# mLSTM cell and exact-GELU block: the values of two batches placed next to each other in the Down stages

## The chip, the cores and the metric

The kernel runs on one core of one Trainium2 chip. The metric is the device time of one execution in microseconds; lower is better. All matmuls are in 32-bit floating point, and each one that the program names appears as two weight loads and two matmul records in the profile.

## What is computed

The first half is an mLSTM cell over 4 batches, 8 heads, 768 time steps and a head size of 40. The second half is a two-layer block with an exact GELU, from 320 features to 2048 and back, applied to the 3072 rows that the first half gives.

```python
for t in range(S):
    m_new  = maximum(f[t] + m, i[t])
    f_stab, i_stab = exp(f[t] + m - m_new), exp(i[t] - m_new)
    C = f_stab * C + i_stab * outer(v[t], k[t])      # 40 x 40 for each batch and head
    n = f_stab * n + i_stab * k[t]
    y[t] = sigmoid(o[t]) * (C @ q[t]) / maximum(abs(n @ q[t]), 1)
x   = y.transpose(0, 2, 1, 3).reshape(3072, 320)
h   = x @ w_in                                        # 320 -> 2048
out = (0.5 * h * (1 + erf(h / sqrt(2)))) @ w_out      # 2048 -> 320
```

## The kernel before

**Chunks and stages.** The sequence is cut into 6 chunks of 128 time steps. Within a chunk the cell is written in its parallel form: scores between all pairs of time steps, weighted, times the values, plus what the carried state gives. The kernel runs in stages. FRONT computes the gates, the cell of chunks 0 and 1 and the products of chunk 0. Then, for c = 1 to 4, an Up stage computes the hidden layer of chunk c, and a Down stage computes the second product of chunk c while the cell of chunk c + 1 runs between its pieces. The text calls these Down stages 1 to 4. A last Up stage and its own product close the kernel. In the profile, the Down stages lie at 155.7 to 197.9, 224.6 to 268.9, 295.6 to 339.2 and 365.8 to 406.6 us.

**What sets the order.** The order within FRONT and DOWN is written out by hand as a string of words; `play` goes through the words and emits the instructions of each. Each engine has its own queue and works through it in that order; it waits where an operand or a buffer is not ready. A word can put instructions on several engines, and on SP, which issues the transfers. No scheduler changes the order.

**The words that matter here.** The digit is the batch.

- `F`: one product step of the Down stage, 8 matmuls of 128 x 128 by 160 columns (L1065). There are 14 in a stage; below they are called F1 to F14 in their order. Two steps fill one bank of PSUM (accumulator memory), then a copy or an addition takes it out (L1076, L1080, L1086).
- `V`: `values`. 8 heads times 4 quarters, 32 matmuls with weights of 128 x 32 and 41 columns (L657), into one bank of tag "a" of the pool `ps_mm`, which has two. One addition on VectorE (DVE) follows (L665). Reading the batch's last inputs also puts loads for the next chunk on a list, `later_loads`, which the next Up stage issues in order.
- `S2`: `scores_two`, the scores of batches 2 and 3 (L555), then 8 multiplications on VectorE (L561). Its four banks are the two of tag "a" and two of tag "tr". `S0` is the same for batches 0 and 1.
- `C2`, `h2`: `read_two` (L610) and `update_two` (L621, and L630, L634, L636 off TensorE) for batches 2 and 3; `C0`, `h0` for batches 0 and 1.
- `K`, `Q`: transposes of keys and queries on VectorE (L489), from the tile `blocks`, which a transfer fills.
- `Z`: pieces of sums of weights on VectorE (L775), in stage 1 only. `N`: two subtractions on VectorE (L1091) that F11 and F12 need.
- `M`, `W`, `G`: mask on GpSimd (POOL, L441), exponentials on ScalarE (ACT, L467), the output gate on ScalarE (L473).
- `Y`: `finish`, on ScalarE, GpSimd and VectorE (L672 to L679). `X`: `turn_y`, 3 transposes on TensorE (L697) and a copy on ScalarE (L707). `R`: `split_x`, two operations on VectorE (L720, L721).

Of the kernel before, what the change touches and what calls it, by code (L numbers as in the profile page):

```python
# [34 lines left out]
    K K B8 F J K F F J K F F F R0 X1 J J K F J F K X2 F J  # L35
    K F J Y3 K F R1 e J F Z B9 B10 F X3 R2 Z R3 F p"""
DOWN = """
    F Z M0 Z W0 F M1 L3 W1 S0 C0 M2 F B3 K2 F G1 h0 Q2 D3 G2 V0 K3 Z W2 F Q3 V1 M3 G0 Z F G3 W3 S2 C2 h2 F Y0 F V2
    F Y1 X0 N Y2 F R0 V3 F X1 F Y3 j X2 R1 F R2 X3 R3 F"""


@with_exitstack
# [1154 lines left out]
```

## Time and profile before

| What | Value |
|---|---|
| median of 3 runs | 465.99 us (465.16 to 466.73) |
| the profiled execution | 465.24 us, span 463.2 us from first to last instruction |
| TensorE matmul (PE), busy | 452.3 us, 98% of the span |
| TensorE weight load (PEld), busy | 400.5 us, 86% |
| VectorE (DVE), busy | 336.7 us, 73% |
| ScalarE (ACT), busy | 253.0 us, 55% |
| GpSimd (POOL), busy | 79.0 us, 17% |
| granted TensorE clock | 1.00 throughout |
| the four Down stages | 42.2, 44.3, 43.6 and 40.7 us |

The busy time of matmuls overlaps from one to the next, so a single row's length is more than what it adds to the path; the step from one start to the next start is what counts. Weight loads run beside matmuls. "Issue" stands for time in which an engine waited for nothing that the profile shows.

### The profile page before, as it was taken

The numbers are of one execution on the slowest core, as the hardware profiler recorded it, in microseconds if no ns is written. First come the engines' busy times: TensorE is split into PE (matmuls) and PEld (weight loads), VectorE is DVE, ScalarE is ACT, GpSimd is POOL, SyncE is SP. The second block draws the span as 40 slices with busy tenths as digits, with TensorE's granted clock in tenths as the row PEclk, the third lists the DMA queues.
The fourth block names the chain that finished last, engine by engine and source line by source line (L and its number), as shares of the span: only waits on it lengthen the run. The fifth ranks groups of instructions, "written<-read, shape, count | busy, mean of one in ns | idle before, by whom it ended". The sixth has DMA issues, their size and how long they took to land.

```text
span 463.2 us, 13002 instructions
## 1 busy us (share of the span) xinstructions
PE 452.3 (98%) x5348; PEld 400.5 (86%) x5348; DVE 336.7 (73%) x737; ACT 253.0 (55%) x545; POOL 79.0 (17%) x120
## 2 busy tenths in 40 slices
PE   8899999999999999999998999999999999999996
PEld 7687888867788899988898998899998899988996
DVE  7899879798868996746577654587664685699950
ACT  6986999854354784203694113594123594257701
POOL 3002120000020232300443200353301411200000
PEclk9999999999999999999999999999999999999999
DMA  9997993268777650057972056973049960210001
GB/s 168 203 215 184 199 224 105 64 135 226 111 201 153 120 98 5 24 115 149 200 124 33 11 118 139 208 112 61 1 87 172 164 106 3 79 38 0 1 1 57
DMA packets 174875, 51.11 MB, mean 110 GB/s; under 512 B 154752, under 2 KB 168352, under 8 KB 174816
## 3 DMA queue, kind: packets, MB, share of 16 engines
q1 hardware_dynamic: 174496, 49.95, 52.9%
q8 instruction: 42, 0.69, 0.6%
q10 hardware_dynamic: 320, 0.33, 0.2%
q14 instruction: 17, 0.14, 0.1%
HBM read 45.47 MB, written 10.03 MB: 120 GB/s over the span
## 4 chain that ended last, share of the span: by engine, by line
PE 89%; DVE 4%; DMA 2%; SPq 1%; POOL 1%; issue 1%; ACT 0%; DVEq 0%; POOLq 0%
PE po L1065 25%; PE pu L949 23%; PE po L1044 7%; PE pu L806 6%; PE pu L960 6%; PE po L919 6%; PE ph L657 4%; PE ps L555 3%; PE pu L812 2%; PE px L697 2%; PE pf L610 1%; PE ps L539 1%; SPq L155 1%; PE pf L577 1%; PE pt L517 1%
## 5 line engine op out<-in xcount | busy, mean ns | idle before, releaser
L1065 PE MATMUL po<-w_out,g 128*128 128x160 f32 x512 | 76.2, 303 | 0.0
L964 ACT ACTIVATE g<-pu 128x512 f32<-128x512 f32 x64 | 32.2, 618 | 77.4 <-PE pu L960 77.4
L1065 PEld LDWEIGHTS po<-w_out,g 128*128 128x128 f32 x512 | 70.3, 190 | 2.2 <-ACT g L964 1.3
L467 ACT ACTIVATE W<-W,aT 128x128 f32<-128x128 f32 x128 | 39.2, 389 | 2.1 <-POOL W L441 2.0
L949 PE MATMUL pu<-x_hi,w_in_hi 128*128 128x512 f32 x160 | 39.0, 387 | 0.0
L441 POOL TENSOR_SCALAR_AFFINE_SELECT W<-W 128x1024 f32<-128x1024 f32 (+2 forms) x20 | 25.0, 1258 | 79.1 <-DMA W<-M_d 70.4
L949 PE MATMUL pu<-x_lo,w_in_lo 128*128 128x512 f32 x160 | 37.8, 379 | 0.0
L1065 PE MATMUL po<-w_sums,sums 128*128 128x160 f32 x256 | 36.9, 302 | 0.0
L1065 PEld LDWEIGHTS po<-w_sums,sums 128*128 128x128 f32 x256 | 35.0, 190 | 0.4
L1044 PE MATMUL po<-w_out,g 128*128 128x320 f32 x128 | 35.2, 433 | 0.0
L686 ACT COPY y_rest<-ob 128x128 f32<-128x128 f32 x16 | 4.8, 298 | 55.4 <-DVE ob L679 29.2
L949 PEld LDWEIGHTS pu<-x_hi,w_in_hi 128*128 128x128 f32 x160 | 29.5, 189 | 5.7 <-ACT g L964 1.3
L949 PEld LDWEIGHTS pu<-x_lo,w_in_lo 128*128 128x128 f32 x160 | 30.2, 189 | 4.3
L526 POOL TENSOR_TENSOR vw<-vb,ewT 128x328 f32<-128x328 f32 x12 | 9.2, 780 | 138.4 <-DMA vb<-in_v_dram 99.2
L1044 PEld LDWEIGHTS po<-w_out,g 128*128 128x128 f32 x128 | 24.0, 190 | 9.6
L949 PE MATMUL pu<-x_all,w_mid 128*128 128x512 f32 x80 | 30.3, 379 | 0.0
L949 PE MATMUL pu<-x_all,w_in_mid 128*128 128x512 f32 x80 | 30.3, 379 | 0.0
L806 PE MATMUL pu<-first_x,w_in 128*128 128x256 f32 x128 | 28.9, 381 | 0.0
L793 DVE TENSOR_TENSOR sums<-g 128x512 f32<-128x512 f32 x16 | 13.6, 853 | 18.3 <-ACT g L964 18.3
L806 PEld LDWEIGHTS pu<-first_x,w_in 128*128 128x128 f32 x128 | 23.8, 190 | 3.3 <-DVE w_in L388 0.2
L765 DVE TENSOR_TENSOR w_in_mid<-w_in_hi,w_in_lo 128x512 fp32r<-128x512 f32 x20 | 13.7, 686 | 16.5 <-PE pu L949 16.5
L561 DVE TENSOR_TENSOR W<-ps,W 128x256 f32<-128x256 f32 (+1 forms) x48 | 17.9, 413 | 10.7 <-PE ps L555 9.0
(196 smaller groups left out, 963.2 us busy)
## 6 DMA issues: line engine op xcount, KB each, us to landing
W<-M_d SPq DMA_DIRECT2D x16, 512.0 KB, 5.6
bits<-in_moe_w_in_dram SPq DMA_DIRECT2D x20, 256.0 KB, 4.5
bits<-in_moe_w_out_dram SPq DMA_DIRECT2D x16, 320.0 KB, 3.2
blocks<-kq_d SPq DMA_DIRECT2D x32, 128.0 KB, 3.3
ob<-in_o_gate_dram SPq DMA_DIRECT2D x24, 160.0 KB, 4.4
out_dram<-o_sb SPq DMA_DIRECT2D x36, 80.0 KB, 2.0
kq_d<-in_k_dram SPq DMA_DIRECT2D x32, 80.0 KB, 2.5
kq_d<-in_q_dram SPq DMA_DIRECT2D x32, 80.0 KB, 2.5
```

Of the source, the lines that this page charges most:

```text
L441: nc.gpsimd.affine_select(out=x, in_=x, compare_op=OP.is_ge, fill=1.0e30, base=base, pattern=[[0, H], [1, x.shape[2]]], channel_multiplier=-1)
L467: nc.scalar.activation(out=W[n][:, h, :], in_=src, func=AF.Exp, scale=-1.0, bias=aT[:, self.c, r:r + 1])
L555: nc.tensor.matmul(ps[i][hip][halves[x ^ i], p, t], kT[i][r, p, halves[x]], qT[i][r, p, t], start=True, stop=True)
L561: nc.vector.tensor_tensor(out=w[r, :, t], in0=ps[i][hip][r, :, t], in1=w[r, :, t], op=OP.mult)
L657: nc.tensor.matmul(ph[r, h, :], Pm[:, h, r], vb[turn_of(n)][:, h, :], start=True, stop=True)
L806: nc.tensor.matmul(banks[-1][e][:, i - i0, :], in_tile(i, x)[:, e, i % 2 * P:(i % 2 + 1) * P], first_x[:, x, t0:t1], start=(x == 0 and i = ...
L919: nc.tensor.matmul(in_pairs(po[t]), x[:, t * L:(t + 1) * L], in_turns(w), start=(f, k) == first, stop=(f, k) == last, skip_group_check=True)
L949: nc.tensor.matmul(in_pairs(pus[i][e]), w[k][:, e, i * P:(i + 1) * P], in_turns(x[:, k, :]), start=(n == 0 and k == 0), stop=False, skip_g ...
L960: nc.tensor.matmul(in_pairs(pu[e]), w[r, i // 2, i % 2 * P:(i % 2 + 1) * P], in_turns(x[r, NX, :]), start=False, stop=(n == 2), skip_group ...
L964: nc.scalar.activation(out=g.t[:, HF * e + i, :], in_=pu[e], func=AF.Gelu, scale=4097.0)
L1044: nc.tensor.matmul(po[b], g.t[:, f, b * L:(b + 1) * L], w_out[:, f, :], start=(f == 0), stop=(f == NF - 1))
L1065: nc.tensor.matmul(bank[k][:, t, :], lhs(j, t), rhs(j), start=(first and t == 0 and j == 0), stop=(t == 1 and j == HF - 1), skip_group_che ...
```

## The change

Only the string DOWN changes. The word `V1` moves from behind `F5` and `Q3` to the place right behind `V0`; the word `V3` moves from behind `F10` and `R0` to the place right behind `V2`. The string is played in all four Down stages, so eight groups of 32 matmuls stand elsewhere in TensorE's order, eight additions elsewhere in VectorE's, and in `later_loads` the entries of `V3` come before that of `X0`. No instruction is added and none removed.

```diff
 DOWN = """
-    F Z M0 Z W0 F M1 L3 W1 S0 C0 M2 F B3 K2 F G1 h0 Q2 D3 G2 V0 K3 Z W2 F Q3 V1 M3 G0 Z F G3 W3 S2 C2 h2 F Y0 F V2
-    F Y1 X0 N Y2 F R0 V3 F X1 F Y3 j X2 R1 F R2 X3 R3 F"""
+    F Z M0 Z W0 F M1 L3 W1 S0 C0 M2 F B3 K2 F G1 h0 Q2 D3 G2 V0 V1 K3 Z W2 F Q3 M3 G0 Z F G3 W3 S2 C2 h2 F Y0
+    F V2 V3 F Y1 X0 N Y2 F R0 F X1 F Y3 j X2 R1 F R2 X3 R3 F"""
```

On TensorE the first junction of a stage was V0 F5 V1 F6 S2 and is now V0 V1 F5 F6 S2. The second was V2 F9 X0 F10 V3 F11 and is now V2 V3 F9 X0 F10 F11.

## The prediction

> **What bounds the kernel now.** I read the page's busy times first, then its chain of waits.
>
> ```profile
> PE 452.3 (98%) x5348; PEld 400.5 (86%) x5348; DVE 336.7 (73%) x737; ACT 253.0 (55%) x545; POOL 79.0 (17%) x120
> ...
> PE 89%; DVE 4%; DMA 2%; SPq 1%; POOL 1%; issue 1%; ACT 0%; DVEq 0%; POOLq 0%
> ```
>
> TensorE holds the path: what shortens its row of instructions counts in full, and so does every hole in it. Next the timeline of PE where Down stage 1 reaches batches 0 and 1 (start, length, line):
>
> ```profile
> 167.16 0.81 PE L621 MATMUL pf<-vw,kb 128*40 128x41 f32 x32
> 167.90 0.81 PE L657 MATMUL ph<-vb,W 128*32 128x41 f32 x64
> 168.65 2.44 PE L1065 MATMUL po<-w_out,g 128*128 128x160 f32 x16
> 171.02 0.81 PE L657 MATMUL ph<-vb,W 128*32 128x41 f32 x64
> ```
>
> L621 is the end of h0, L657 is V0 and V1, L1065 between them is the product step F5; F6 follows V1 and S2 starts at 174.13. By differences of starts V0 takes 0.74, F5 2.37, V1 0.74, F6 2.37. There is no hole. A V is dense: 64 weight loads and 64 matmuls in 0.74 us, where an F has 32 such instructions in 2.37.
>
> The same timeline in stage 3 has holes. A bracket gives the idle time before a row, and "issue" means that nothing in the profile was being waited for:
>
> ```profile
> 310.93 0.56 PE L657 MATMUL ph<-vb,W 128*32 128x41 f32 x34
> 311.89 0.50 PE L657 MATMUL ph<-vb,W 128*32 128x41 f32 x30 [0.40 <-issue]
> ...
> 316.08 0.49 PE L610 MATMUL pf<-state,qT 64*64 64x41 f32 x18
> 316.99 0.90 PE L610 MATMUL pf<-state,qT 64*64 64x41 f32 x46 [0.42 <-issue]
> ```
>
> Start to start the two holes are 0.60 and 0.65 us; stage 2 has one of 0.65 (247.28 to 247.94, in h2), and the cell in FRONT one of 0.64 (92.68 to 93.31, in a V). I counted TensorE's records (loads, matmuls, its own waits) from the trace's start: these four stops fall on instructions 2,241, 5,825, 7,361 and 7,617, which are 193 above a multiple of 256, all four. The page's third part gives the unit:
>
> ```profile
> q8 instruction: 42, 0.69, 0.6%
> ```
>
> 42 packets of 16 KB for 10,788 instructions, so a packet is a block of 256. So the stops are TensorE waiting for its own instructions. In the DMA view the block ahead of each stop starts at 90.83, 245.65, 309.62 and 314.55 and is copied in 1.10, 0.93, 0.88 and 1.09; TensorE goes on at 93.31, 247.94, 311.89 and 316.99. From the end of the copy that is 1.38, 1.36, 1.39 and 1.35 us: **a block can be used about 1.37 us after its copy ends**. A block is asked for some 300 instructions before its first is needed (copies never start earlier than that, and 0.5 to 3.5 us after TensorE passes that point). 300 instructions with an F among them last over 4 us; three dense groups in a row don't.
>
> **The change, part by part.** No instruction is added or removed; in each of four Down stages V1 goes in front of F5 and V3 in front of F9.
>
> *Fewer changes of shape (gain).* F5 and F6 in one run take 4.54 (as the runs of two in all stages do) instead of 2 x 2.37: -0.20. V0 is followed by V1 instead of F5. Its 64 matmuls last 0.615 from first start to last start, and the step to F5 is 0.13. The step V to V is not in the trace: the nearest row with equal tile shapes (L555 to L610) has 0.04, a change of shape (L621 to L657) 0.13, the pitch inside a V 0.01. I take 0.04: V0 costs 0.65, -0.09. First junction -0.29 (bounds -0.20 and -0.32). At the second, V2 likewise -0.09, F10 goes from 2.27 to 2.18 because F11 follows it, F11 from 2.28 to 2.18 because no V precedes it: -0.28.
>
> *Where the first junction's gain is lost.* In stage 2 S2 waits:
>
> ```profile
> 244.46 1.45 PE L555 MATMUL ps<-qT,kT 64*64 64x128 f32 x56 [1.00 <-DVE far L665]
> ```
>
> The releaser is V1's addition on VectorE, queued behind K3 and Q3, which came late since K2 waited for its transfer. With V1 in front of K3 the addition comes first and Q3 last: the same three pieces of work end at 244.41 as before, and S2 needs Q3. TensorE only waits longer: 0 in stage 2 (bound -0.29, if the stop in h2 shrinks).
>
> *Instruction blocks (cost).* Instruction numbers within the moved pieces shift, so a boundary meets other work. I laid the new order over the count.
> Stage 1: instruction 3,521 (13 x 256 + 193) is now the 117th of V1's 128. V1 starts at 167.90 + 0.65 = 168.55 and reaches it at 169.1. Its block is asked for in h0, before anything changes; it starts at 168.58 and is copied in 1.43, so it is there at 168.58 + 1.43 + 1.37 = 171.38. Before, V1 came to the same number at 171.41, just late enough. Stop: 2.27 us (1.75, if the distance from the copy's start, 2.27 at the shortest stop, is what counts). From V0 to S2: 0.65 + 0.56 + 2.27 + 0.17 for V1's rest + 4.54 = 8.19 against 6.23: +1.96.
> Stage 3: instruction 7,361 is the 104th of V1, reached at 307.82 + 0.65 + 0.50 = 308.97; its block is usable at 311.89, as the trace shows: a stop of 2.92. V0 to S2: 0.65 + 0.50 + 2.92 + 0.24 + 4.54 = 8.85 against 6.87 (which held the old 0.60): +1.98. The next boundary (7,617, in C2) is reached at 318.3; its block was usable at 316.99, so the old 0.65 goes: -0.65.
> Stages 2 and 4: the boundaries lie in S2 (5,569, usable 1.37 after 239.77) and early in V1 (9,153, reached at 378.2; its block, started at 373.88 and copied in 0.88, is usable at 376.1). No stop.
> Second junctions: V2 and V3 follow two F and nothing dense. The tightest is stage 1, instruction 4,289, early in F10, some 4.4 us after V2's start, where its block was asked for; that block took 1.1 to start, 1.31 to copy and 1.37 to be used, 3.8 together. No stop, at 0.6 us of slack.
>
> The Trainium skill has a rule against these stops. Its page "Runtime: NRT & Kernel Launch", section "Instruction fetch mechanics", says that instructions come in 16 KiB blocks of 256, that TensorE holds 2,048 of them, and that crossing a block is "mostly hidden". The block size agrees with the 42 packets; the four stops, about 300 instructions after a request, speak against both the depth and the hiding. By that rule the sum would be the gains alone, which is the first rival.
>
> *Queues.* On VectorE V1's addition (0.46 to 0.50) now stands before K3, the pieces of Z and Q3. In stage 4 Q3 ends at 381.55 instead of 381.09, and S2 starts at 383.28; in stages 1 and 3 the stopped V1 lets Q3 end near 174.3 and 314.2, before S2 at 176.1 and 316.7. Cost 0, up to the stop's whole length again if F5 and F6 (4.54) did not cover it. V3's addition stands before Y1, N and Y2. In stage 4 VectorE sits idle 0.57 before Y1's multiplication, waiting for GpSimd (393.08); the addition fits there. N ends at 395.84, and F11, which reads its first half at once and its second half 1.06 us later, starts at 396.4: 0. V1 and V3 put nothing on ACT or POOL. V1's inputs have been ready since 376.02 in stage 4 (S0's last product on VectorE; V1 now 377.99), V3's since 389.76 (V3 now 390.9): no new wait. On SP, V3's later loads stand ahead of X0's load of `ob`, some 3 us of issue in the next Up stage; in stage 2 that load was issued at 223.27 and G0 reads it at 241.65: 0.
>
> **Sum.** Second junctions 4 x -0.28 = -1.14; first junction in stage 4 -0.29; stage 1 +1.96; stage 3 +1.98 - 0.65; stage 2 0: **+1.86 us**. The profiled execution took 465.24 us (span 463.2, 2.0 around it), which would become 467.1. It lies 0.75 below the median of the three runs, 465.99; on that the forecast is 467.85, written 467.8. With the bounds of each term (stops 1.75 and 2.4, junctions 0.20 to 0.32) the case runs from 466.6 to 469.2.
>
> **Rivals.**
> 1. *No stops* (blocks arrive in time): the gains alone, 7 x -0.29, and the old 0.60 goes too where its boundary is met without a stop: 465.99 - 2.0 to -2.7, about 463.6. For it: only four stops in 42 blocks. Against it: both blocks in question are asked for before the change acts, and TensorE arrives 2 to 3 us before they were usable. It decides if a block starts under about 0.3 us after it is asked for. Chance 0.14.
> 2. *One stop, or two half as long*: the delay from request to start varies from 0.5 to 3.5 us in the trace. With one stop of 2 us left, -2.0 - 0.6 + 2.0 gives 465.4; two halved ones 465.7 to 466.5. Chance 0.27.
> 3. *Longer stops*: a block delayed like the slowest (3.5 + 1.4 + 1.4 = 6.3 us after request, against 1.9 us from request to need in stage 1) would stop V1 4.4 us there: 470.0. Chance 0.09.
> 4. The forecast, 0.50.
>
> **How the numbers follow.** Predicted is the likeliest case, 467.8. The range reaches from the upper part of rival 1 to short of rival 3's far end: 464.2 to 469.4. About 0.3% (1.4 us) is what a measurement of this kernel can tell from no change. Slower by more than that: nearly all of the forecast's case and of rival 3, 0.57. Faster: rival 1 and a little of rival 2, 0.16. Between: 0.27.
>
> **What the profile would show.** Right: in stages 1 and 3 PE's timeline splits the second of the two adjacent L657 groups, with "issue" and over 1.5 us; the C2 hole of stage 3 is gone; F5 and F6 are one row of x32 lasting 4.6; stage 2's wait of S2 now ends on Q3 (L489) and is longer. Wrong: V0 and V1 run through in 1.4 us in stage 1, or TensorE's stops no longer sit at 193 above a multiple of 256, or S2 is held by VectorE in stages 1, 3 or 4.

## The result and the profile after

Six runs of the changed kernel gave a median of 469.77 us (468.18 to 471.20), six of the kernel before on the same chip 465.71 us (464.86 to 466.73). The ratio is 1.0087, interval 1.0059 to 1.0115: slower, by 4.06 us where 1.86 was forecast. The direction and the mechanism of the stops were right; the forecast size was less than half of the measured one. Three runs of the whole case (one of `first_only`, one of `bridge`, one of before beside `first_only`) were 12 to 66% longer at a mean granted clock of 0.85 or less and are left out of every time below.

The profiled execution took 471.13 us with a span of 469.2. First the page, with its busy row and its chain of waits:

```profile
PE 454.1 (97%) x5348; PEld 403.0 (86%) x5348; DVE 338.9 (72%) x737; ACT 253.5 (54%) x545; POOL 77.7 (17%) x120
...
PE 89%; DVE 6%; issue 2%; DMA 1%; ACT 1%; SPq 0%; POOL 0%; DVEq 0%
```

The same instructions, and TensorE still holds the path. "Issue" has doubled from 1% to 2%. The timeline of PE at the first junction of stage 1 shows where:

```profile
169.10 0.81 PE L621 MATMUL pf<-vw,kb 128*40 128x41 f32 x32
169.84 1.49 PE L657 MATMUL ph<-vb,W 128*32 128x41 f32 x121
172.83 0.28 PE L657 MATMUL ph<-vb,W 128*32 128x41 f32 x7 [1.50 <-issue]
173.04 4.61 PE L1065 MATMUL po<-w_out,g 128*128 128x160 f32 x32
```

V0 and V1 are 128 matmuls in one row, and 7 from its end TensorE stops for 1.70 us from start to start. The instruction behind the stop is number 3,521. Stage 3 has the other stop, at 7,361:

```profile
311.12 0.81 PE L621 MATMUL pf<-vw,kb 128*40 128x41 f32 x32
311.86 1.52 PE L657 MATMUL ph<-vb,W 128*32 128x41 f32 x113
315.32 0.50 PE L657 MATMUL ph<-vb,W 128*32 128x41 f32 x15 [1.94 <-issue]
315.75 6.04 PE L1065 MATMUL po<-w_out,g 128*128 128x160 f32 x32
321.73 1.57 PE L555 MATMUL ps<-qT,kT 64*64 64x128 f32 x64
```

2.14 us from start to start. Nothing is split in C2 behind it: the old stop at 7,617 is gone. But F5 and F6 last 6.04 here and 4.61 in stage 1. The reason is in the windows of that stretch (busy time and instructions of PE, PEld, DVE, ACT and POOL, then the granted clock):

```profile
315.28:318.69 3.41, 3.37 (x26) 3.27 (x26) 3.34 (x9) 1.87 (x3) 0.00 (x0) 0.50 0.93 210
318.69:322.00 3.31, 3.31 (x32) 3.14 (x34) 0.88 (x2) 0.17 (x1) 1.74 (x2) 1.00 0.45 52
```

From 315.28, where TensorE goes on, the granted clock is 0.50 for 3.41 us. That was in no term of the sum.

In the table below, a Down stage runs from its first product matmul to the first matmul of the next Up stage, and every entry is the difference from the profile of before (42.21, 44.32, 43.58 and 40.73 us). "K2" is the start of that transpose within stage 2, which its transfer sets.

| Kernel | Down 1 | Down 2 | Down 3 | Down 4 | K2 |
|---|---|---|---|---|---|
| before | 0 | 0 | 0 | 0 | 13.58 |
| after | +1.49 | +0.61 | +2.18 | -0.14 | 14.14 |
| first_only | +1.52 | -1.13 | +0.96 | -0.08 | 12.43 |
| second_only | -0.08 | -0.12 | -0.61 | -0.03 | 13.51 |
| after_16 | -0.07 | -0.51 | -0.41 | -0.16 | 13.05 |
| before_16 | 0.00 | -0.60 | -0.32 | 0.00 | 13.65 |
| after_up16 | -0.28 | -1.95 | -1.04 | -0.17 | 12.19 |
| after_up16b | -0.28 | -1.82 | -0.22 | -0.17 | 12.43 |
| before_up16 | 0.00 | -1.15 | +0.29 | 0.00 | 12.69 |
| before_up28 | +0.32 | -1.44 | -0.02 | 0.00 | 11.97 |
| bridge | -0.07 | +0.78 | -0.92 | +0.04 | 14.04 |
| swapped_up16 | +0.04 | +0.99 | +0.45 | -0.61 | 14.61 |
| mixed_up16 | -0.50 | +0.65 | +0.02 | -0.39 | 15.19 |
| mixed_loads | -0.50 | -0.81 | -0.79 | -0.36 | 13.76 |

The Up stages and the last product change by 0.01 us at most, apart from 0.23 (16 matmuls) or 0.44 (28) that some of these kernels add there. FRONT, which the change doesn't touch, is 1.94 us longer in the profile of after and 1.86 in that of second_only; both show a granted clock of 0.66 from 14 to 19 us, where first_only shows 1.00. The order of words in FRONT is the same in all three, so it belongs to the execution. The Down stages of after sum to +4.14 us.

### The profile page after: what moved, and what is told of

Its sections match the earlier page's. It is cut to its first block, busy times and chain, and to the rows that moved or that the text cites. A ratio compares the mean times of both kernels' runs of the same rounds, so it can differ in the third digit from the quotient of the medians.

```text
span 469.2 us, 13008 instructions
## 1 busy us (share of the span) xinstructions
PE 454.1 (97%) x5348; PEld 403.0 (86%) x5348; DVE 338.9 (72%) x737; ACT 253.5 (54%) x545; POOL 77.7 (17%) x120
## 4 chain that ended last, share of the span: by engine, by line
PE 89%; DVE 6%; issue 2%; DMA 1%; ACT 1%; SPq 0%; POOL 0%; DVEq 0%
PE po L1065 26%; PE pu L949 22%; PE po L1044 7%; PE pu L960 6%; PE po L919 6%; PE pu L806 5%; PE ph L657 4%; PE ps L555 3%; PE ps L539 2%; PE pf L610 2%; PE px L697 2%; PE pu L812 2%; PE pf L621 1%; DMA blocks<-kq_d 1%; PE pt L517 1%
## 5 line engine op out<-in xcount | busy, mean ns | idle before, releaser
L1065 PEld LDWEIGHTS po<-w_out,g 128*128 128x128 f32 x512 | 71.5, 193 | 1.8 <-ACT g L964 1.3
L1044 PEld LDWEIGHTS po<-w_out,g 128*128 128x128 f32 x128 | 24.0, 190 | 9.6
```

Source lines behind the costliest of these rows:

```text
L1044: nc.tensor.matmul(po[b], g.t[:, f, b * L:(b + 1) * L], w_out[:, f, :], start=(f == 0), stop=(f == NF - 1))
L1065: nc.tensor.matmul(bank[k][:, t, :], lhs(j, t), rhs(j), start=(first and t == 0 and j == 0), stop=(t == 1 and j == HF - 1), skip_group_che ...
```

## The experiments

The theory was that V1 directly behind V0 runs into a block of instructions that isn't there yet, and that this alone turns a small gain into a loss. The rivals were that VectorE, a buffer or a load makes TensorE wait, or that the two V side by side cost more by themselves.

**One junction at a time.** `first_only` moves V1 alone:

```diff
-    ... G2 V0 K3 Z W2 F Q3 V1 M3 ...
+    ... G2 V0 V1 K3 Z W2 F Q3 M3 ...
```

> V1 behind V0, V3 left where it was. Theory A (TensorE waits for blocks of instructions; the step from V to V costs 0.25 us instead of 0.04): stops again on instructions 3,521 (stage 1) and 7,361 (stage 3), 1.5 to 2.9 us each, the C2 stop of stage 3 gone; stage 4 ends its first junction 0.1 us earlier. Time +3 to +5 us over the kernel before, nearly all of the change. Rival B (the loss is spread over all eight junctions, through the additions moved ahead on VectorE): about half of the change, +2 us, and half of it in stages 2 and 4.

`second_only` moves V3 alone:

```diff
-    ... F V2 F Y1 X0 N Y2 F R0 V3 F ...
+    ... F V2 V3 F Y1 X0 N Y2 F R0 F ...
```

> V3 behind V2, V1 left where it was. Theory A: no boundary falls into dense work, so no new stop; F10 and F11 gain 0.2 and the V to V step loses 0.2 a stage: within 0.6 us of the kernel before; the three old stops (instructions 5,825, 7,361, 7,617) stay. Rival B: the other half of the change, +2 us.

On one chip `first_only` took 468.43 us, `second_only` 465.44 and before 464.8: ratios 1.0084 (1.0053 to 1.0115) and 1.0005 (0.9974 to 1.0036). The loss is in the first junction. Its stops stand at 3,521 (1.70 us) and 7,361 (2.39 us) again, in the timeline of PE of stage 3:

```profile
308.10 1.54 PE L657 MATMUL ph<-vb,W 128*32 128x41 f32 x114
311.83 0.35 PE L657 MATMUL ph<-vb,W 128*32 128x41 f32 x14 [2.19 <-issue]
312.11 4.61 PE L1065 MATMUL po<-w_out,g 128*128 128x160 f32 x32
```

Here the stop is longer than in after, and yet F5 and F6 last 4.61 at a clock of 1.00. The second junction should have brought 0.28 us a stage; in stages 1 and 4, where nothing else changed, it brought 0.08 and 0.03.

**The same order on other blocks.** If the boundaries are the cause, moving them must remove the stops without touching the order. Sixteen added matmuls of one column (64 instructions for TensorE), ahead of nearly everything, do that. `after_16` is after with this edit, `before_16` is before with it:

```diff
+    few = ps_h.tile([P, P], F32, name="few", tag="h")
+    for _ in range(16):
+        nc.tensor.matmul(few[:, 0:1], w_out[:, 0, 0:P], w_out[:, 0, 0:1], start=True, stop=True, skip_group_check=True)
```

> The changed kernel, with 16 matmuls of one column put in at the very start, which shift every later TensorE instruction by 64 numbers. Theory A: instructions 3,521 and 7,361 now are others, in h0 and C2; no stop over 0.3 us in any Down stage, no drop of the clock in stage 3; each of stages 1 and 3 shorter by 1.5 to 2.2 us than in the changed kernel; time 464.5 to 466.5 (the extra matmuls cost up to 1 us at the start). Rival C (V1 itself waits, for its values, its weights or its bank, and the numbers are chance): the stops stay in V1 and the time stays within 1 us of the changed kernel.

> The kernel before with the same 16 matmuls. Theory A: its three stops of 0.60 to 0.65 in Down stages 2 and 3 go as well, one of up to 0.7 may come in stage 2; Down stages together 1 to 2 us shorter, whole time -1.5 to +0.5 us. Rival C: the stops stay where they are, time +0 to +1 us.

As whole times these two missed: 469.6 and 470.72 us (ratios 1.0111 and 1.0124), because FRONT became 6.21 and 7.17 us longer. The traces show where that comes from: matmuls of 128 x 128 follow each other every 0.213 us until 16.14 us in `after_16` and every 0.111 us from then on, while in before the step falls at 5.50 us. The first granted clock of 1.00 is recorded at just these two times. So TensorE ran at half its rate 10.6 us longer, and the "1.00 throughout" of the table for before holds from 5.50 us on. Why the one-column matmuls do that was not tested. In the Down stages the pair says what was asked: both stops in V1 are gone, and stages 1 and 3 fall from +1.49 and +2.18 to -0.07 and -0.41. One stop of 0.61 us, at 5,825 in C2 of stage 2 of `after_16`, was not expected.

The expectation also had the places wrong: 3,521 and 7,361 still fall into V1, 64 instructions nearer its start. What changed is what lies in front of them. In after, h0, V0 and V1 up to the boundary of stage 1 are 64 + 128 + 116 = 308 instructions, so the point 300 ahead lies in h0; moved by 64 they are 244, and that point lies in the product steps before h0, which take 4.5 us.

So the same 64 instructions went to the start of the first Up stage, where they cost 0.23 us: `after_up16` on after, `before_up16` on before, and 28 matmuls (112 instructions) in `before_up28`, which should put other boundaries of before into dense work.

```diff
+            for i in range(16 if c == 1 and f == 0 else 0):
+                r = quarters[i % 4]
+                nc.tensor.matmul(pus[0][0][r, 0:1], ident[:, r], ident[:, 0:1], start=True, stop=True, skip_group_check=True)
```

> The changed kernel, with the 64 extra TensorE instructions (16 matmuls of one column with weights of 32 columns) at the start of the first Up stage, so that FRONT is untouched and its warm-up too. Theory A (blocks of instructions): stages 1 and 3 lose their stops as with the shift at the start; the extra matmuls cost 0.3 to 0.6 us; time within 0.8 us of the kernel before. Rival C (V1 itself waits): +3 to +4.5 us, as the changed kernel.

> The kernel before with the same 64 instructions. Theory A: Down stages 2 and 3 lose 0.6 and 0.3 us as with the shift at the start, the extra matmuls cost 0.3 to 0.6: -0.6 to +0.3 us. The difference from the shifted changed kernel, with no stops in either, is what the new order itself is worth: -0.5 to +0.2 us.

> The kernel before in its own order, with 112 extra instructions. Theory A: now the boundary falls into C2 of stages 1 and 3, behind S2 with nothing wide between: stops of 0.7 to 1.8 us there, in L610, on instructions 193 above a multiple of 256; Down stages 1 and 3 together +0.7 to +3 us over before, without any change of order. Rival C: Down stages unchanged.

Measured: 462.87, 464.5 and 465.16 us, against 464.44 for before; ratios 0.9977 (0.9960 to 0.9993), 1.0009 (0.9993 to 1.0025) and 1.0021 (0.9998 to 1.0044). The timeline of PE in `after_up16`, stage 1:

```profile
167.08 0.81 PE L621 MATMUL pf<-vw,kb 128*40 128x41 f32 x32
167.82 1.56 PE L657 MATMUL ph<-vb,W 128*32 128x41 f32 x128
169.31 4.61 PE L1068 MATMUL po<-w_out,g 128*128 128x160 f32 x32
```

V0 and V1 run through, and the Down stages have no stop at a block. For 3,521 the copy now starts 0.81 us before h0; in after it started 1.40 us behind the start of h0. The changed order without its stops is 0.2% below before, where with them it is 0.9% above: the stops, with what follows them, are the loss. Against `before_up16`, the same shift in the old order, it is 1.6 us faster, more than the 0.5 us expected; in the profile of `before_up16` both old stops of stage 3 are gone, but S2 waits 1.50 us there, so that the stage is 0.29 us longer than in before. `before_up28` confirmed the unit and missed place and size. New stops appear at instructions 4,033, 5,569 and 7,873, all 193 above a multiple of 256: right behind h2 of stage 1, in V1 of stage 2 and in h2 of stage 3. They last 0.37, 0.48 and 0.64 us, and those that I expected in C2 are not there. A repeat of `after_up16` was to narrow its interval:

> The shifted changed kernel once more, for comparison on the same chip: 1 to 2 us under the kernel before.

It gave 464.19 us against 464.90, ratio 0.9993 (0.9970 to 1.0015). So about 0.1 to 0.2% faster, less than the 1 to 2 us expected; that this version beats before is shown in one of the two comparisons only.

**Density.** If a stop needs several dense groups in a row, one F in front of V0 should remove it with the boundary still in V1. `bridge` is after with F5 moved there, without added matmuls:

```diff
-    ... h0 Q2 D3 G2 V0 V1 K3 Z W2 F Q3 M3 ...
+    ... h0 Q2 D3 G2 F V0 V1 K3 Z W2 Q3 M3 ...
```

> The changed kernel with one word moved: F5 stands in front of V0 instead of behind V1 (h0, F5, V0, V1, F6). No extra instructions, V0 and V1 still adjacent. Theory A: the boundary still falls into V1 (instructions 3,521 and 7,361), but 2.37 us of F5 now lie between asking for the block and needing it, so the stop of stage 1 goes (4.4 us against some 3.8) and that of stage 3 is 0 to 1 us, as in the kernel before. F5 and F6 are no longer one run (+0.2 a stage), the V steps cost as in the changed kernel. Time +0.2 to +1.8 us over the kernel before, 2 to 4 us under the changed kernel. Rival C (V1 directly behind V0 is what stops it): stops as in the changed kernel, +3 to +4.5 us.

```profile
166.49 0.81 PE L621 MATMUL pf<-vw,kb 128*40 128x41 f32 x32
167.24 2.44 PE L1065 MATMUL po<-w_out,g 128*128 128x160 f32 x16
169.61 1.57 PE L657 MATMUL ph<-vb,W 128*32 128x41 f32 x128
171.11 2.44 PE L1065 MATMUL po<-w_out,g 128*128 128x160 f32 x16
```

This is the timeline of PE, stage 1: h0, F5, V0 and V1 in one row, F6. V1 runs through in stages 1 and 3 with the boundary in it, since F5's 2.37 us now lie between the request and the need. The stop at 5,825 in h2 of stage 2 stays and lasts 1.08 us here. 465.06 us against 464.9, ratio 1.0001 (0.9976 to 1.0025): one word's place decides over the loss.

**The step from V to V.** Without stops, stage 1 of `after_up16` gains 0.28 us where the forecast for both junctions together was 0.57. The source view of L657 in after, at the second junction of stage 1 (PEldq is the sequencer that feeds TensorE):

```profile
L657 PE MATMUL ph<-vb,W x64: 197/200/224, 185.3 to 185.9; 128*32 128x41 f32 x64
L657 PE MATMUL ph<-vb,g x64: 197/199/224, 186.2 to 186.8; 128*32 128x41 f32 x64
L657 PEldq EVENT_SEMAPHORE  x3: 51/51/51, 185.8 to 186.1; - x3
```

Three wait instructions of the second V stand in the queue between its matmuls and those of the first. In the eight places of after, the last start of the first V and the first of the second are 0.25 us apart in five, 0.31 and 0.28 in two (three waits in each of these), and 0.14 in the one with two waits. None of them waits for anything late; from two waits to three the step grows by 0.107 us. If that is the price, the batch whose operands need fewer waits should come second. `swapped_up16` is after with both pairs turned and the 64 instructions of `after_up16`:

```diff
-    ... V0 V1 ... V2 V3 ...
+    ... V1 V0 ... V3 V2 ...
```

> The changed kernel with 64 extra instructions and with V1 in front of V0 and V3 in front of V2. Theory D (the step from V to V is the second V's wait instructions on TensorE's own queue, 0.11 us each, which no F hides now): the second V now has its values from one transfer instead of two, so one wait less, and the step is 0.14 instead of 0.25 us in all eight places; stages shorter by 0.1 to 0.2 each than in the shifted changed kernel, 0.7 us in all. Rival E (a change of weights, values or bank on TensorE): the step stays 0.25.

The step fell to 0.013 to 0.035 us in seven places and 0.093 in one, with no or one wait in between: the theory holds, beyond the number expected. But the time is 464.87 us against 464.44, ratio 1.0020 (1.0000 to 1.0039). V1 in front waits for its weights, 1.74 us from start to start in stage 2 and 1.20 in stage 3. The timeline of PE, stage 2:

```profile
236.86 0.81 PE L621 MATMUL pf<-vw,kb 128*40 128x41 f32 x32
239.25 0.50 PE L657 MATMUL ph<-vb,W 128*32 128x41 f32 x32 [1.57 <-ACT W L467]
239.99 1.63 PE L657 MATMUL ph<-vb,W 128*32 128x41 f32 x96 [0.24 <-DVE W L561]
```

I took that for the price of V1 in front, so that only the second pair should be turned. `mixed_up16` is `after_up16` with V3 V2:

```diff
-    F V2 V3 F Y1 X0 N Y2 F R0 F X1 ...
+    F V3 V2 F Y1 X0 N Y2 F R0 F X1 ...
```

> The shifted changed kernel with V3 in front of V2, V0 in front of V1. Theory D: at the second junction the step from V to V falls from 0.25 to 0.03 us, since V2 brings one wait of its own instead of three; V3's weights, ready 0.8 to 1.5 us before V2 starts, are in time, so nothing is lost for it. 0.2 us a stage, 0.8 us in all, under the shifted changed kernel. Rival F (V3 in front waits for its weights, as V1 in front did in stages 2 and 3): 0 to 2 us slower than it.

It took 465.38 us against 464.9, ratio 1.0013 (0.9995 to 1.0032): not faster. The second junction steps in 0.03 in all stages and stage 1 gains 0.50, but in stage 2 V1 again waits, 1.61 us:

```profile
239.04 0.81 PE L657 MATMUL ph<-vb,W 128*32 128x41 f32 x64
241.27 0.51 PE L657 MATMUL ph<-vb,W 128*32 128x41 f32 x32 [1.41 <-DVE W L561]
```

The order of the words is also the order of `later_loads`: with V3 first, its loads go ahead of V2's on SP. `mixed_loads` keeps V3 V2 and sorts the list by batch (the first line stands behind two of the appends):

```diff
+                later_loads[-1].turn = b
...
+        later_loads.sort(key=lambda x: getattr(x, 'turn', B))
```

> mixed_up16 with the loads of batch 2 issued before those of batch 3 again, as in the kernel before; the order of the products is V0 V1 and V3 V2, the 64 records at the start of the first Up stage stay. Theory G: in mixed_up16 the 1.6 us that V1 of stage 2 waited for its weights came from the turned order of the loads, which put the mask tile of batch 1 behind that of batch 2 on the load queue. Then here that wait is gone (V0 to V1 about 0.25 again in stage 2, no wait on W above 0.5), V3 to V2 stays at 0.03, Down stage 2 is 1 to 2 us shorter than in mixed_up16, and the time is 0.5 to 1.5 us below that of mixed_up16, which is 1 to 2.5 us below the kernel before (ratio 0.995 to 0.998). Rival: the late weights are a matter of when the transfers happen to land, not of their order; then the wait can come in any stage and the time is that of mixed_up16 (ratio 1.000 to 1.002).

463.19 us against 464.72, ratio 0.9965 (0.9941 to 0.9988), and stage 2 is 1.46 us shorter than in `mixed_up16`. The first GpSimd work of stage 2 in the timelines of `mixed_up16` and of `mixed_loads`:

```profile
233.46 0.74 POOL L526 TENSOR_TENSOR vw<-vb,ewT 128x328 f32<-128x328 f32 x1 [37.65 <-PE pf L610]
```

```profile
227.31 0.76 POOL L526 TENSOR_TENSOR vw<-vb,ewT 128x328 f32<-128x328 f32 x1 [33.48 <-DMA vb<-in_v_dram]
```

The expectation named the wrong tile. What came late was `vb` of the pair of batches (issued at 227.9 against 223.3), on which GpSimd's first operation waits; the masks, the exponentials and V1's weights queue behind it. In the first line the named releaser, L610, stands in for that transfer: its group begins only at 232.73, and `mixed_loads` runs the same operation before C0 has started. The order of the loads was the cause, as far as one profile of each shows it, and this version is faster than before, by 0.1 to 0.6%. `swapped_up16` turned its loads too: it issued the same `vb` at 226.7, 1.35 us behind the start of stage 2, where before, after and `mixed_loads` issue it 1.5 to 2.7 us ahead of it. So its wait may have the same cause, and V1 in front with sorted loads was not run.

## Why the prediction was wrong in size

**Right.** The stops fell on exactly the two instructions that the count named, 3,521 and 7,361, in V1 of stages 1 and 3; the one in C2 went; stages 2 and 4 had none in V1. The other boundary, 5,825 in h2 of stage 2, kept its stop (0.80). F5 with F6 take 4.55 us in stage 1 and F10 with F11 4.35, as summed. In stage 2 S2 waits longer and for Q3, as the waits of TensorE's weight loads in that stage (total, times, longest) show, first of before, then of after:

```profile
PEld ps L555 <- DVE far L665: 1.4, 2, 1.2
```

```profile
PEld ps L555 <- DVE qT L489: 1.0, 1, 1.0
PEld ps L555 <- DVE far L665: 0.9, 2, 0.7
```

Rival 1 fell: the page "Runtime: NRT & Kernel Launch" of the Trainium skill, section "Instruction fetch mechanics", has TensorE hold 2,048 instructions and calls a crossing "mostly hidden"; two crossings here cost 1.70 and 2.14 us, and moving the boundaries by 64 instructions removed both.

**Wrong.** Two steps of the prediction failed. "I take 0.04" priced the step from V to V by the change of shape alone; it measured 0.14 to 0.31 because of the waits in the queue. And the sum put F5 and F6 behind a stop at 4.54, so it gave the clock after a stop no cost; in stage 3 they took 5.98 at half the clock. Term by term, on the Down stages' +4.14:

1. *The step V to V.* "I take 0.04", from the nearest row with equal tile shapes. It measured 0.14 to 0.31, above its upper bound of 0.13. The row had the shape right, but no wait instruction stands between L555 and L610, where two or three stand between V and V. By stage +0.37 (both junctions of stage 1), +0.21 (stage 2, second only), +0.42, +0.45: +1.45 us. Where the step is 0.03, the forecast gain appears: stage 4 of `swapped_up16` has -0.61 against the forecast -0.57.
2. *The clock behind the stop.* 1.44 us (F5 and F6 in 5.98 instead of 4.54) that no term had. Over the runs: after took 468.4 us in the two at a mean clock of 1.00, 469.8 in two at 0.996 and 471.2 in two at 0.992, steps of 1.4 each. Six of nine runs of `first_only` were at 0.996 or less, against 17 of 99 of before and 7 of 36 of `after_up16`, its repeat and `mixed_loads`. But 5 of 10 of `second_only`, whose stops are short, were too, and a mean does not tell the stage: three of the profiles have such a stretch in FRONT. That the stops bring the halved clock is likely and not shown. The runs at a clock of 1.00 are 2.7 us above before's median, and so are the Down stages without this term.
3. *The stops' size.* 1.70 instead of 2.27, as the copy took 0.93 us instead of 1.43; 2.14 instead of 2.92, as the block started 1.24 us after h0's start instead of 2.54, which outweighed a longer copy (1.35 for 0.88) and a later use (1.61 us behind the copy instead of 1.39). Together -1.35 us. Some of it is term 1 again: V1 reached the boundary 0.10 and 0.21 us later because of the longer step, and the stop was shorter by that much. The durations of one execution's copies are no constants.
4. *Stage 2.* Given 0 for the first junction. K2's transfer landed 0.56 later within the stage, and S2 is released by K2 plus 6.3 us in both orders. K2 starts at 11.97 to 13.65 us in the profiles that keep V3 in its old place and at 12.19 to 14.14 in those with V3 behind V2, so the 0.56 is probably the execution and not the order; one program profiled twice gave 12.19 and 12.43. The gain of 1.1 to 2.0 us in some kernels' stage 2 is for the most part an earlier K2 as well. The stop in h2 grew from 0.65 to 0.80, +0.15.

The terms: 1.88 as summed by stage, +1.45, +1.44, -1.35, +0.56 and +0.15, give 4.13. Two misses of opposite sign, the step and the stops' size, hid each other by chance; the clock and stage 2 are what shows. The range ended 0.4 us short: it bounded the stops, which came out smaller, and held neither the step above 0.13 nor the clock.

## What to carry to other kernels

A reorder on a saturated engine moves its instruction boundaries too: count the instructions from the start, lay the multiples of the block over the new order, and look at the 300 or so in front of each boundary. Where they are all dense groups, as h0, V0 and most of V1 were here, expect a stop; one sparse group among them removed both long stops, and so did 64 filler instructions ahead. Between two dense groups count the second one's wait instructions, not the change of tile shape alone. And where issue order of loads follows the order of compute words, turning two words turns their loads: sort them separately.

## What the runs showed of the hardware that was not expected

- A wait instruction that is already fulfilled takes 51 ns by its record. Two dense groups of matmuls stand 0.013 us apart with none between them and mostly 0.035, 0.14 and 0.25 us with one, two and three, so each beyond the first adds about 0.107 us.
- The granted clock went to 0.50 for 3.41 us after a hole of 2.14 us in after, and stayed at 1.00 after one of 2.39 us in `first_only`. The Trainium skill's page "TensorE: Matmul & The Clock Gate", section "Why this matters for your kernels", warns of idle gaps above some 3 us: here a shorter one stood in front of a halved window, in some executions only.
- Within a trace the stretches of one recorded clock all last a multiple of 3.41 us (in after 10.24, 3.41, 296.96, 3.41 and 150.19), so they lie on a grid. One step of the grid, 311.87 to 315.28, holds the whole hole of after: matmuls are busy in 1.46 us of it, and the next step is halved. So it is in stage 2 of `swapped_up16`, with 1.61 us busy and a halved step from 240.36. The longer hole of `first_only` is split over two steps with 2.10 and 2.49 us busy, and neither is followed by a halved one. So the place of a hole on this grid may decide. It is not shown: near the end of `second_only` a step with 1.44 us busy was followed by a clock of 1.00.
- In after a block of 256 instructions was usable 1.39 to 1.61 us after its copy ended, and the copies in front of its stops took 0.93 to 1.35 us. The stop at 2,241 in FRONT, with the same instructions ahead of it in every kernel but the `_16` pair, lasted from 0.24 us in `bridge` to 0.96 us in `second_only`.
